# Normalising the probabilities of the first eight attention units on ScalarE and VectorE in place of GpSimd

## The chip, the core and the metric

The program runs on one core of a Trainium2 chip. The metric is the device time of one execution in microseconds (us). Five engines run their own queues in order: TensorE (PE; its weight loads are listed apart as PEld), VectorE (DVE), ScalarE (ACT), GpSimd (POOL) and SyncE (SP), which issues nearly all DMAs.

## What is computed

An attention with a forget gate, and two MLPs behind it, in float32:

```
attn:  scale*q@k.T + min(-(cum_i - cum_j), 0), causal, softmax, @ v      4 batches, 8 heads, 576 positions, 64 columns
x   -> moe:   g = s*relu(x@w_in)^2 + b;               x = g@w_out        2304 x 512, hidden 2048
x   -> moe2:  g = max(h,0) + alpha*min(h,0), h=x@w_in; out = g@w_out     2304 x 512, hidden 2048
```

`cum` is the running sum of max(s, 0). The softmax is `exp(scores - max) / (sum + 1e-9)`; the division is what the change moves.

## The kernel before

**Attention.** The work is cut into 32 units: a batch, a pair of heads, and one of two ranges of rows (rows 0 to 319 or 320 to 575). Range 0 has three row blocks, of 64, 128 and 128 rows with 64, 192 and 320 keys. Range 1 has two blocks of 128 rows, with 448 and 576 keys. The first eight units are called native: they use plain float32 matmuls. Units 0 to 3 (range 0 of batch 0) are early too: they borrow buffers of weights that are not there yet. Units 4 to 7 are range 1 of batch 0.

For each head of a unit `scores` fills the tile `probs` with the gate's bias (on ScalarE at L431 for the second head of a native unit, on VectorE at L435 for all others), masks it on GpSimd (L439), multiplies q and k (L457), combines score and bias with a running minimum or maximum on VectorE (L461), and takes the exponential on ScalarE with its sum (L473). Then VectorE adds 1e-9 and takes the reciprocal of the sums (L480, L481), and one GpSimd instruction for each row block scales `probs` by it in place (L484). `values` turns the scaled blocks with TensorE (L515, tile pt), copies them to `pf` (L519, on ScalarE and on VectorE), multiplies with v (L531) and copies the result into the MLP's input `xf` (L546, ScalarE).

**MLPs.** Each of the 16 packets of weights is converted from 64-bit to 32-bit numbers (L140 on ScalarE, L141 and L142 on VectorE) and split in a high and a low part (L130 on ScalarE, L131 on VectorE or GpSimd). A block of 256 tokens of the first MLP runs an up product (L783), the activation (L802 to L804, the split at L130 and L131) and a down product (L897) for each packet.

**Order.** The program starts with attention alone, up to the point where units 0 to 3 are done and unit 4 has begun. This stretch, some 62 us, is called the prelude here. In it TensorE also runs filler matmuls on zeros (`busy`, L97), which are kept at their place in the order. Then the first block of the MLP starts, and in it units 4 to 8 run beside the conversion of packets 4 to 15. Attention goes on beside later blocks until about 546 us; the second MLP takes the rest. The order on each engine is not that of the text: line 1047 asks for a planner that simulates the engines with its own costs and writes out each engine's queue from that. On the chip the queues run in that fixed order. Another mix of instructions gives another plan.

Of the kernel before, what the change touches and what calls it, by code (L numbers as in the profile page):

```python
# [12 lines left out]
AF = mybir.ActivationFunctionType  # L13
ALU = mybir.AluOpType
# [5 lines left out]
def tile_forget_attention__then__two_mlps(  # L20
# [20 lines left out]
    nc = tc.nc  # L41
# [52 lines left out]
    def busy(n):  # L94

        for _ in range(n):
            tc.keep_in_program_order(nc.tensor.matmul(scratch, dense[:, :P], dense, start=True, stop=True))  # L97
# [306 lines left out]
    def scores(u, h):  # L404

        own = HALF[h]
        head = u.b * H + u.h0 + h
        flip = u.native and h == 1
        nr = len(u.blocks)
        nm = two.tile([P, 3], F32, tag="nm", name=f"nm_{u.tag}_{h}")  # L410
        sm = two.tile([P, 3], F32, tag="sm", name=f"sm_{u.tag}_{h}")
        if u.rng == 0:
            nc.gpsimd.memset(sm[:, 0:1], 1.0)
        big = None if u.early else two.tile([P, 1088], F32, tag="probs", name=f"probs_{u.tag}_{h}")
        probs, col = {}, 0
        for r in u.blocks:
            i0, i1 = IB[r]
            rows = i1 - i0
            if u.early and r != 1:
                big, col = u.buf(two, 0, F32, "", f"probs{h}{r}"), 0  # L420

            width = -(-i1 // P) * P if i1 < S else S
            pt = probs[r] = big[:, col : col + width]
            col += width
            if width > i1:
                nc.gpsimd.memset(pt[:, i1:], 0.0)
            if r == 0:
                nc.gpsimd.memset(pt[64:P, 0:64], 0.0)

            if flip:  # L430
                nc.scalar.activation(  # L431
                    pt[:rows, :i1], u.cums[h][:rows, :i1], AF.Relu, scale=-1.0, bias=cumT[:rows, r, head : head + 1]
                )
            else:
                nc.vector.tensor_scalar(  # L435
                    out=pt[:rows, :i1], in0=u.cums[h][:rows, :i1], scalar1=cumT[:rows, r, head : head + 1],
                    scalar2=0.0, op0=ALU.subtract, op1=ALU.min,
                )
            nc.gpsimd.affine_select(  # L439
                out=pt[:rows, i0:i1], in_=pt[:rows, i0:i1], pattern=[[-1, rows]], base=0,  # L440
                channel_multiplier=1, compare_op=ALU.is_ge,
                fill=-MASKED if flip else MASKED,
            )
        u.probs[h] = probs
        for m, r in enumerate(u.blocks):
            i0, i1 = IB[r]
            rows, n = i1 - i0, i1
            a0 = i0 - u.q0
            pt = probs[r]
            init = -KEEP_ALL if flip else KEEP_ALL  # L450
            for j0, j1 in ([(0, n)] if n <= 512 else [(0, 320), (320, n)]):
                sc = u.bank("sc", f"sc{h}_{r}_{j0}")

                scr, all_ = sc[:rows, : j1 - j0], sc[:, : j1 - j0]
                aq = slice(a0, a0 + P)
                if u.native:
                    nc.tensor.matmul(all_, u.qk[0][own, aq], u.qk[1][own, j0:j1], start=True, stop=True)  # L457
                else:
                    nc.tensor.matmul(all_, u.xs[h][0][:, aq], u.xs[h][1][:, j0:j1], start=True, stop=False)
                    nc.tensor.matmul(all_, u.ql[h][:, aq], u.xs[h][1][:, j0:j1], start=False, stop=True)  # L460
                nc.vector.tensor_tensor_reduce(  # L461
                    out=pt[:rows, j0:j1], in0=scr, in1=pt[:rows, j0:j1], scale=SCALE if flip else -SCALE, scalar=init,
                    op0=ALU.subtract if flip else ALU.add, op1=ALU.max if flip else ALU.min,
                    accum_out=nm[:rows, m : m + 1],
                )
                if u.n < EARLY:
                    busy(1)
                init = nm[:rows, m : m + 1]
            if flip:
                nc.vector.tensor_scalar(  # L470
                    out=nm[:rows, m : m + 1], in0=nm[:rows, m : m + 1], scalar1=-1.0, scalar2=None, op0=ALU.mult
                )
            nc.scalar.activation(  # L473
                pt[:rows, :n], pt[:rows, :n], AF.Exp, bias=nm[:rows, m : m + 1], scale=1.0 if flip else -1.0,
                accum_out=sm[:rows, m : m + 1],
            )
            yield
        if u.n == 0:
            busy(4)
        nc.vector.tensor_scalar(out=sm[:, :nr], in0=sm[:, :nr], scalar1=1e-9, scalar2=None, op0=ALU.add)  # L480
        nc.vector.reciprocal(sm[:, :nr], sm[:, :nr])  # L481
        for m, r in enumerate(u.blocks):
            rows, n = IB[r][1] - IB[r][0], IB[r][1]
            nc.gpsimd.tensor_scalar(  # L484
                out=probs[r][:rows, :n], in0=probs[r][:rows, :n], scalar1=sm[:rows, m : m + 1],
                scalar2=1.0, op0=ALU.mult, op1=ALU.mult,
            )
        yield

    def values(u, h):  # L490
# [73 lines left out]
    def attention():  # L564
# [22 lines left out]
        for u in us:  # L587
            split_v(u)
        yield from transpose_qk(us[0])
        yield from alternate(transpose_qk(us[1]), scores(us[0], 0))  # L590
        yield from alternate(transpose_qk(us[2]), scores(us[0], 1))
        yield from alternate(transpose_qk(us[3]), scores(us[1], 0), values(us[0], 0))
        yield from alternate(scores(us[1], 1), values(us[0], 1))
        yield from alternate(scores(us[2], 0), values(us[1], 0))
# [457 lines left out]
```

## Time and profile before

| | |
|---|---|
| time, median of 3 runs | 1039.78 us (1039.27 to 1041.05) |
| the profiled execution | 1040.97 us; span from first to last instruction 1039.2 us |
| PE busy | 1019.4 us, 98% |
| DVE busy | 681.3 us, 66% |
| ACT busy | 672.4 us, 65% |
| POOL busy | 457.6 us, 44% |
| L484, POOL, whole execution | 160 instructions, 91.0 us |

Busy time is the sum of an engine's instructions. The idle time of an engine that is not the bottleneck costs nothing. "Idle before <- X" is the time in which an engine had nothing to run, and the instruction whose end let it go on. [...]

### The profile page before, as it was taken

What the parts mean: (1) busy time and instruction counts of PE and PEld (TensorE: products, weight loads), DVE (VectorE), ACT (ScalarE), POOL (GpSimd) and SP (SyncE); (2) the same over time, 40 slices, a digit from 0 to 9 for tenths busy, and PEclk for the clock granted to TensorE, in tenths of its full rate; (3) what the DMA queues carried; (4) which work ended last, traced back from release to release, by engine and by line L of the source; (5) the groups of instructions that cost most, each with busy time, mean ns of one, the idle gap of its engine ahead of it and who ended that gap; (6) DMA issues with size and microseconds to landing.
All of it is one profiled execution on the core that took longest, in us unless ns stands there. A gap on an engine that the chain in (4) does not pass through costs nothing. (4 is left out here: it accounts for less than half of the span.)

```text
span 1039.2 us, 20636 instructions
## 1 busy us (share of the span) xinstructions
PE 1019.4 (98%) x6952; PEld 925.8 (89%) x6952; DVE 681.3 (66%) x1605; ACT 672.4 (65%) x1669; POOL 457.6 (44%) x876
## 2 busy tenths in 40 slices
PE   9899999999999999999999999999999999999997
PEld 4568899999999999999999888888899999999996
DVE  6979865787676776677655865857665456455443
ACT  5877876777787877778776776645454455445433
POOL 5656775666677666777562000574611011001000
PEclk9999999999999999999999999999999999999999
DMA  7988433343232432334215762645644335334331
GB/s 167 255 211 239 132 68 70 71 93 79 40 92 64 102 72 52 79 68 91 66 35 173 240 192 74 207 147 170 196 163 142 103 112 172 103 99 136 104 104 46
DMA packets 197930, 125.45 MB, mean 121 GB/s; under 512 B 138496, under 2 KB 167936, under 8 KB 197824
## 3 DMA queue, kind: packets, MB, share of 16 engines
q1 hardware_dynamic: 193744, 123.56, 42.8%
q8 instruction: 55, 0.90, 0.4%
q10 hardware_dynamic: 4080, 0.57, 0.3%
q14 instruction: 51, 0.42, 0.1%
HBM read 106.19 MB, written 17.90 MB: 119 GB/s over the span
## 5 line engine op out<-in xcount | busy, mean ns | idle before, releaser
L783 PE MATMUL hp<-xh,w 128*128 128x256 f32 (+1 forms) x1024 | 229.0, 300 | 0.3 <-ACT r L802 0.3
L907 PE MATMUL acc<-w,ring 128*128 128x512 f32 x864 | 214.6, 392 | 1.1 <-DVE ring L131 0.7
L907 PEld LDWEIGHTS acc<-w,ring 128*128 128x128 f32 x864 | 155.8, 188 | 29.3 <-DVE ring L131 1.1
L783 PEld LDWEIGHTS hp<-xh,w 128*128 128x128 f32 x1024 | 171.4, 189 | 6.2 <-ACT r L802 0.5
L897 PE MATMUL acc<-gh,w 128*128 128x256 f32 x896 | 172.4, 286 | 0.5 <-ACT res L926 0.5
L783 PE MATMUL hp<-xl,w 128*128 128x256 f32 (+1 forms) x512 | 152.6, 298 | 0.0
L897 PEld LDWEIGHTS acc<-gh,w 128*128 128x128 f32 x896 | 136.0, 189 | 3.2 <-issue 1.6
L883 POOL TENSOR_TENSOR cc<-u,t 128x256 f32<-128x256 f32 x32 | 26.1, 817 | 235.5 <-DVE u L874 201.5
L897 PE MATMUL acc<-gl,w 128*128 128x256 f32 x448 | 118.7, 288 | 2.2 <-POOL gl L131 2.2
L484 POOL TENSOR_SCALAR probs<-probs,sm 64x64 f32<-64x64 f32 (+4 forms) x160 | 91.0, 581 | 60.5 <-DVE sm L481 49.9
L473 ACT ACTIVATE probs<-probs,nm 64x64 f32<-64x64 f32 (+4 forms) x160 | 90.0, 563 | 38.5 <-DVE nm L461 32.7
L131 POOL TENSOR_TENSOR gl<-r,gh 128x256 fp32r<-128x256 f32 x112 | 89.5, 799 | 48.6 <-ACT gh L130 42.1
L817 PE MATMUL p<-xs,sums 128*128 128x256 f32 x768 | 104.7, 282 | 0.4 <-DVE u L859 0.4
L783 PEld LDWEIGHTS hp<-xl,w 128*128 128x128 f32 x512 | 97.1, 190 | 3.3 <-issue 0.4
L817 PEld LDWEIGHTS p<-xs,sums 128*128 128x128 f32 x768 | 98.0, 189 | 2.1 <-DVE u L859 0.6
L461 DVE CUSTOM_DVE_ANT_0 probs<-sc,probs 128x320 f32<-128x320 f32 (+3 forms) x160 | 68.2, 427 | 41.2 <-PE sc L460 32.8
L817 PEld LDWEIGHTS p<-xs,w 128*128 128x128 f32 x576 | 79.0, 189 | 8.7 <-DVE u L874 2.0
L802 ACT ACTIVATE r<-hp 128x256 f32<-128x256 f32 (+1 forms) x144 | 58.0, 403 | 44.1 <-PE hp L783 33.2
L817 PE MATMUL p<-xs,w 128*128 128x256 f32 x576 | 82.3, 282 | 2.4 <-DVE u L874 1.5
L897 PEld LDWEIGHTS acc<-gl,w 128*128 128x128 f32 x448 | 80.1, 188 | 5.0 <-POOL gl L131 2.8
L828 DVE SCALAR_TENSOR_TENSOR ph<-pl,misc,ph 128x512 f32<-128x512 f32 x64 | 51.7, 807 | 42.4 <-ACT pl L844 42.4
L515 PE MATMUL pt<-ident,probs 128*128 128x128 f32 x480 | 74.3, 275 | 4.6 <-POOL probs L484 4.4
(149 smaller groups left out, 2116.8 us busy)
## 6 DMA issues: line engine op xcount, KB each, us to landing
sums<-sums_d SPq DMA_DIRECT2D x128, 256.0 KB, 2.7
wi<-in_moe_w_in_dram SPq DMA_DIRECT2D x32, 512.0 KB, 4.7
wo<-in_moe_w_out_dram SPq DMA_DIRECT2D x32, 512.0 KB, 4.8
cum<-cum_d SPq DMA_DIRECT2D x32, 288.0 KB, 3.7
sums_d<-w SPq DMA_DIRECT2D x64, 128.0 KB, 1.8
cum<-cum_d SPq DMA_DIRECT2D x30, 160.0 KB, 3.0
nat<-in_k_dram SPq DMA_DIRECT2D x64, 72.0 KB, 2.5
x_d<-res SPq DMA_DIRECT2D x18, 256.0 KB, 2.2
```

Of the source, the lines that this page charges most:

```text
L131: lo_eng.tensor_tensor(out=lo, in0=src, in1=hi.bitcast(F32), op=ALU.subtract)
L461: nc.vector.tensor_tensor_reduce(out=pt[:rows, j0:j1], in0=scr, in1=pt[:rows, j0:j1], scale=SCALE if flip else -SCALE, scalar=init, op0=AL ...
L473: nc.scalar.activation(pt[:rows, :n], pt[:rows, :n], AF.Exp, bias=nm[:rows, m : m + 1], scale=1.0 if flip else -1.0, accum_out=sm[:rows, m ...
L484: nc.gpsimd.tensor_scalar(out=probs[r][:rows, :n], in0=probs[r][:rows, :n], scalar1=sm[:rows, m : m + 1], scalar2=1.0, op0=ALU.mult, op1=A ...
L515: nc.tensor.transpose(tp[:, o : o + P], u.probs[h][r][:, k0 : k0 + P], ident)
L783: nc.tensor.matmul(hs, a[:, c], b[c], start=(n == 0), stop=(n == len(terms) * NCC - 1))
L802: relus.append(nc.scalar.activation(r, hs, AF.Relu, scale=1.0 / W_SCALE).ins)
L817: nc.tensor.matmul(bank, lhs[:, c * P : (c + 1) * P], rhs[:, c], start=(start and c == 0 and z == 0), stop=(c == 1 and z == 2), skip_group ...
L828: nc.vector.scalar_tensor_tensor(out=r, in0=u, scalar=nalpha[:, f : f + 1], in1=r, op0=ALU.mult, op1=ALU.add).ins
L883: nc.gpsimd.tensor_tensor(out=cc[:, T:], in0=u3, in1=t5, op=ALU.add)
L897: nc.tensor.matmul(banks[d] if count == 2 else acc[d // 2][:, d % 2], a[:, d * P : (d + 1) * P], b, start=(f == 0 and (d % 2 == 0 or count ...
L907: nc.tensor.matmul(banks[m], a[:, m * P : (m + 1) * P], b, start=(f == 0 and b is woh and a is gh), stop=(f == NF - 1 and a is gl),)
```

## The change

For native units, GpSimd's scaling is replaced: the first head of the pair (h = 0) is scaled by ScalarE with an activation (Copy with the reciprocal as a per-row scale), the second (h = 1) by VectorE with a tensor_scalar multiplication. All other units keep GpSimd.

```
         for m, r in enumerate(u.blocks):
             rows, n = IB[r][1] - IB[r][0], IB[r][1]
-            nc.gpsimd.tensor_scalar(
-                out=probs[r][:rows, :n], in0=probs[r][:rows, :n], scalar1=sm[:rows, m : m + 1],
-                scalar2=1.0, op0=ALU.mult, op1=ALU.mult,
-            )
+            pt, by = probs[r][:rows, :n], sm[:rows, m : m + 1]
+            if not u.native:
+                nc.gpsimd.tensor_scalar(out=pt, in0=pt, scalar1=by, scalar2=1.0, op0=ALU.mult, op1=ALU.mult)
+            elif h:
+                nc.vector.tensor_scalar(out=pt, in0=pt, scalar1=by, scalar2=None, op0=ALU.mult)
+            else:
+                nc.scalar.activation(pt, pt, AF.Copy, scale=by)
```

## Rows read from the trace of the kernel before

**Rows 1.** Busy time in stretches: start:end, length, each engine's busy (instructions), PEclk, DMA.
```profile
0.00:62.00 62.00, 55.52 (x227) 30.85 (x228) 48.27 (x159) 40.91 (x116) 35.95 (x112) 0.94 0.87 213
62.00:137.00 75.00, 73.80 (x490) 62.73 (x489) 67.11 (x138) 60.14 (x145) 49.99 (x73) 1.00 0.68 178
...
30.00:40.00 10.00, 9.33 (x38) 5.61 (x38) 9.47 (x34) 9.44 (x31) 5.19 (x12) 0.87 0.80 211
40.00:50.00 10.00, 8.85 (x44) 5.65 (x43) 9.56 (x30) 9.51 (x26) 5.29 (x9) 0.96 1.08 260
```
**Rows 2.** Timeline of PE around the prelude's end: start, length, instruction, [idle before].
```profile
53.76 0.55 PE L515 MATMUL pt<-ident,probs 128*128 128x128 f32 x3 [2.79 <-POOL probs L484]
...
60.51 1.30 PE L531 MATMUL av<-pf,vn 128*128 128x320 f32 x6
...
61.67 0.47 PE L783 MATMUL hp<-xh,w 128*128 128x256 f32 x1
```
**Rows 3.** Timeline of POOL, the scaling of four heads in the prelude.
```profile
23.34 1.53 POOL L484 TENSOR_SCALAR probs<-probs,sm 64x64 f32<-64x64 f32 x3 [0.72 <-DVE sm L481]
...
31.87 1.21 POOL L484 TENSOR_SCALAR probs<-probs,sm 64x64 f32<-64x64 f32 x3 [1.09 <-DVE nm L470]
...
34.55 1.57 POOL L484 TENSOR_SCALAR probs<-probs,sm 64x64 f32<-64x64 f32 x3 [1.15 <-DVE sm L481]
...
52.69 1.52 POOL L484 TENSOR_SCALAR probs<-probs,sm 64x64 f32<-64x64 f32 x3
```
**Rows 4.** Timeline of DVE, the reciprocal of unit 3's second head.
```profile
51.59 0.25 DVE L480 TENSOR_SCALAR sm<-sm 128x3 f32<-128x3 f32 x1
...
52.36 0.16 DVE L481 RECIPROCAL sm<-sm 128x3 f32<-128x3 f32 x1
```
**Rows 5.** Timeline of ACT: a trio and a pair at L431, an exponential's end.
```profile
14.22 1.15 ACT L431 ACTIVATE probs<-cum,cumT 64x64 f32<-64x64 f32 x3
...
47.08 0.19 ACT L473 ACTIVATION_READ_ACCUMULATOR probs<-probs,nm 128x1 f32 x1
...
72.64 1.34 ACT L431 ACTIVATE probs<-cum,cumT 128x448 f32<-128x448 f32 x2
```
**Rows 6.** Busy time of L484's instructions alone, in two stretches.
```profile
0.00:62.00 62.00, 13.00 (x26) 0.94 0.87 213
62.00:137.00 75.00, 12.40 (x14) 1.00 0.68 178
```
**Rows 7.** Timeline of DVE, multiplications of these shapes at L435.
```profile
13.70 1.66 DVE L435 TENSOR_SCALAR probs<-cum,cumT 64x64 f32<-64x64 f32 x3
...
23.41 1.64 DVE L435 TENSOR_SCALAR probs<-cum,cumT 64x64 f32<-64x64 f32 x3
...
26.71 2.68 DVE L435 TENSOR_SCALAR probs<-cum,cumT 64x64 f32<-64x64 f32 x3
...
65.44 0.86 DVE L435 TENSOR_SCALAR probs<-cum,cumT 128x448 f32<-128x448 f32 x2
...
154.46 0.77 DVE L435 TENSOR_SCALAR probs<-cum,cumT 64x64 f32<-64x64 f32 x3
```
**Rows 8.** Timeline of DVE, one instruction of the conversion, at three places.
```profile
32.29 1.08 DVE L141 TENSOR_SCALAR wt<-wt 128x512 uint32<-128x512 uint32 x1 [0.50 <-ACT wt L140]
...
35.50 0.90 DVE L141 TENSOR_SCALAR wt<-wt 128x512 uint32<-128x512 uint32 x1
...
43.55 0.39 DVE L141 TENSOR_SCALAR wt<-wt 128x512 uint32<-128x512 uint32 x1
```
**Rows 9.** PE alone in stretches of 2 us: busy, PEclk, DMA.
```profile
54.00:56.00 2.00, 2.00 (x10) 0.61 1.06 360
56.00:58.00 2.00, 2.00 (x8) 0.53 1.14 157
```
**Rows 10.** What L484 waited for in the prelude: us in total, times.
```profile
DVE sm L481: 7.2, 5
```
**Rows 11.** Table loads of ACT in the whole execution.
```profile
L84 ACT ACT_TABLE_LOAD x1 | 1.3, 1283 | 1.2 <-PEq L1034 1.2
```

## The prediction

> **What bounds the kernel now.** Read first the busy time in two stretches [rows 1]: the prelude (0 to 62 us) and the MLP's first block with units 4 to 7 beside it (62 to 137 us). From 62 us TensorE is busy for 73.80 of 75 us at full clock, and the whole span has it at 98%. So behind the prelude the kernel is bound by TensorE's own work, which the change leaves alone, and a microsecond is won there only by taking one of the 1.2 us of its idle time. The prelude is different: TensorE is idle for 6.5 us of it and spends much of the rest on filler matmuls. What lasts longest there is seen in its middle [rows 1]: from 30 to 50 us VectorE is busy for 19.03 us of 20 and ScalarE for 18.95, while GpSimd has 10.48.
>
> Read next, backwards from the first MLP matmul at 61.67 us, what TensorE did [rows 2]. Before it stands the product with v of unit 3's second head at 60.51. Earlier is the longest stall of the prelude: TensorE stood for 2.79 us, until 53.76, for GpSimd's scaling of that same head, and everything behind those transposes, the product of the first head included, stood with it. GpSimd had started at 52.69 [rows 3], at once behind the reciprocal that VectorE ran at 52.36 [rows 4]. VectorE ran the addition in front of it at 51.59, though ScalarE had finished that head's last exponential at 47.27, which is 47.08 + 0.19 [rows 5]: 4.3 us in VectorE's queue. The end of the prelude therefore hangs on two things, how long VectorE's queue takes to reach that reciprocal, and the scaling step behind it.
>
> **The change part by part.** *What GpSimd loses.* The scaling of units 0 to 7 is 13.0 us in the prelude and 12.4 us behind it [rows 6], 25.4 us in all, and none of it stands on GpSimd's own limit: that engine has idle time in both stretches.
>
> *The last scaling of the prelude (unit 3, second head) goes to VectorE.* Before, from the reciprocal's end (52.52) to the end of GpSimd's three instructions (52.69 + 1.52 = 54.21) was 1.69 us. The trace has no such multiplication by a reciprocal on VectorE. The nearest is L435, the same instruction type on the same three shapes, in and out of SBUF: 0.77 us for the trio where nothing slows it, 1.64 and 1.66 where GpSimd works beside it, 2.68 at worst [rows 7]. I take 0.77, because the GpSimd work that is removed is what often stood beside it, and because the row at 0.77 stands for 13 trios of that length in the trace. No semaphore of another engine stands between the reciprocal and this multiplication. The step gets shorter by 1.69 - 0.77 = 0.92 us. Bounds: 0.92 less, or 0.99 more (2.68).
>
> *VectorE's queue in front of it.* Three more second heads (units 0, 1, 2) are scaled before 52 us: 3 x 0.77 = 2.31 us longer. Against this stands what GpSimd's scaling costs VectorE today. L141 takes 0.39 us alone, and 1.08 and 0.90 while GpSimd scales from 31.87 to 33.08 and from 34.55 to 36.12 [rows 3, 8], 0.69 and 0.51 more. The trios of 1.66 and 1.64 us at L435 lie 0.89 and 0.87 above 0.77, the second beside the scaling at 23.34 [rows 3, 7]. These four places make 2.96 us. The queue is then 2.31 - 2.96 = 0.65 us shorter. GpSimd's other work moves into the room and will slow some of the same instructions, so I count half, 0.3 us shorter. Bounds: nothing removed and trios at 1.64 (4.9 us longer), or the whole 0.65 shorter.
>
> [...]
>
> *First heads go to ScalarE.* Nearest is L431, a ScalarE instruction on the same shapes with a per-row operand: 1.15 us for three blocks, 1.34 for two [rows 5]. Four trios make 4.6 us and four pairs 5.4. In the prelude unit 0's trio falls where ScalarE is idle; the trios of units 1, 2 and 3 go into the full queue, 3.45 us in front of the last exponential that now ends at 47.27. What hides it is the 4.3 us that this exponential's result lies in VectorE's queue; 0.85 us of that cover is left. If VectorE's queue got shorter by more than that, ScalarE would be late next, and the gain of the queue stops there. Unknown functions cost nothing: the trace has one table load in the whole execution [rows 11], and it already holds a plain copy beside the exponential.
>
> ScalarE also takes over the wait for the reciprocal. Queued behind it are exponentials, casts of weights and copies of pf; VectorE waits for the first two, TensorE for the last. I cost the wait at nothing, because the planner puts the scaling behind work that is ready; the second rival prices the opposite.
>
> *Behind the prelude.* Units 4 to 7 put 4 x 0.86 = 3.4 us on VectorE (the pair at 65.44 [rows 7]) and 4 x 1.34 = 5.4 us on ScalarE. Their idle time between 62 and 137 us is 75 - 67.11 = 7.9 us and 75 - 60.14 = 14.9 us [rows 1]; this covers both, and TensorE is fed from work done ahead. I cost it at nothing. Without that cover it would be up to 3.4 us. DMAs, their queues and their order in the text stay; the change issues none.
>
> *Sum.* -0.92 - 0.3 = -1.2 us. Against the profiled execution, 1040.97 us (span 1039.2 and 1.8 around it), that is 1039.8. The median of the runs lies 1.19 us below the profiled one, so I forecast 1039.78 - 1.2 = 1038.6 us.
>
> **The rivals.** A difference under 0.2% (2.1 us) is about what a measurement of this kernel can't tell from none.
>
> *The prelude's stall goes altogether (faster).* The planner writes the order anew. If it puts unit 3's addition and reciprocal 3 us nearer to the exponential, for which 4.3 us are there, the stall of 2.79 us is gone [rows 2]. [...] An engine that hasn't stood may keep its clock. Together 2.79 + 1.7 = 4.5 us: 1035.3. For it: VectorE's queue loses foreign waits, and two queues now hold the scaling that one held. Against it: the filler matmuls keep their places, and from 30 to 40 us, where TensorE is idle for 0.67 us alone, the granted clock is 0.87 too [rows 1].
>
> *ScalarE stands in front of the reciprocals (slower).* GpSimd waited five times for L481 in the prelude, 7.2 us in all, 1.44 each [rows 10]. It had nothing else to do; ScalarE has. If the plan places the scaling too early for units 1, 2 and 3, ScalarE stands 3 x 1.44 = 4.3 us between 23 and 47 us, with exponentials behind it. 0.85 us is covered, 3.4 is not, VectorE waits for the exponentials and gains nothing from its shorter instructions. -0.92 + 3.4 = +2.5 us: 1042.3. It decides from 0.85 + 0.92 = 1.8 us of waiting on. For it: ScalarE has 1.05 us of idle time in 20 [rows 1]. Against it: no planner that sees the reciprocal's time need put anything ahead of it.
>
> *The new multiplications are held as L435 is today.* Trios at 1.64 us: 3 x 1.64 - 2.96 = +2.0 us in the queue, and the last step 1.64 against 1.69. About +1.9 us: 1041.7. For it: two of the three prelude trios shown are at that price [rows 7]. Against it: 13 us of GpSimd's work are gone from the same stretch [rows 6].
>
> **How the numbers follow.** The forecast's case has 0.40, the case without the stall 0.35, ScalarE's waits 0.17, the held multiplications 0.08. Faster by over 0.2%: 0.35 and 0.02 from the edge of the forecast's case, 0.37. Slower: 0.17 and 0.01 from the edge of the held ones, 0.18. Within 0.2%: 0.38 and 0.07, 0.45. The range goes from 1034.8, half a microsecond under the case without the stall, to 1041.9, just above the held multiplications; it leaves out most of ScalarE's case. The forecast's own range is 1037.6 to 1040.2.
>
> **What the profile after would show.** The first L783 matmul at about 60.5 us instead of 61.67; L484 on GpSimd only from unit 8 on; trios near 0.8 us on VectorE and 1.15 on ScalarE; L141 nearer to 0.39 before 50 us; TensorE's stall in front of unit 3's second transposes under 2 us, now ended by VectorE; still about 1.2 us of idle time on TensorE between the prelude's end and 137 us. The prediction is wrong if the first L783 matmul comes after 62 us, if ScalarE waits for L481 for more than 1.8 us in the prelude, if the clock stays full through the prelude's end, or if the new plan moves idle time of TensorE into the first block or later ones.

## The result and the profile after

The changed kernel takes 1051.72 us in the median of 6 runs (1049.77 to 1054.42); the kernel before took 1039.88 beside it. The ratio is 1.0113 (1.0096 to 1.0131): 12 us slower, where 1.2 us less were forecast and the range ended at 1041.9. The profiled execution is 1052.57 us, span 1050.8. Lines behind L490 are shifted by 3: L518 is the transposes (L515 before), L522 the copy of pf (L519), L534 the product with v (L531), L786 and L900 the up and down products (L783, L897), L805 and L807 the activation (L802, L804). L490 is the scaling on ScalarE, L488 that on VectorE.

TensorE's timeline at the prelude's end in the changed kernel (start, length, instruction, [idle before]), to be set beside [rows 2]:

```profile
48.91 0.38 PE L97 MATMUL acc_first<-dense 128*128 128x512 bf16 x1
53.96 0.88 PE L518 MATMUL pt<-ident,probs 128*128 128x128 f32 x3 [4.67 <-ACT probs L490]
54.76 3.78 PE L457 MATMUL sc<-turned 64*128 64x448 f32 x6
...
68.14 1.20 PE L534 MATMUL av<-pf,vn 128*128 128x320 f32 x6
...
69.20 0.47 PE L786 MATMUL hp<-xh,w 128*128 128x256 f32 x1
```

The first up product starts 7.53 us later than in [rows 2]. TensorE goes on at nearly the same time as before (53.96 and 53.76), but it had waited for something else: for unit 3's *first* head, where before it was the second. All of unit 3's transposes and products then still lay ahead, and the six score matmuls of unit 4, which had run in front of the stall (at 49.01, in 1.96 us), came behind it and took 3.78 us.

Why the first head was late is seen on VectorE and ScalarE: the end of the first head's exponential, then the addition and the reciprocal (L480, L481), and the scaling. Before, the first head:

```profile
40.41 0.20 ACT L473 ACTIVATION_READ_ACCUMULATOR probs<-probs,nm 128x1 f32 x1
...
42.73 0.15 DVE L480 TENSOR_SCALAR sm<-sm 128x3 f32<-128x3 f32 x1
...
43.47 0.15 DVE L481 RECIPROCAL sm<-sm 128x3 f32<-128x3 f32 x1
```

After, ScalarE:

```profile
45.85 0.19 ACT L473 ACTIVATION_READ_ACCUMULATOR probs<-probs,nm 128x1 f32 x1
...
53.13 1.14 ACT L490 ACTIVATE probs<-probs,sm 64x64 f32<-64x64 f32 x3
```

After, VectorE (51.11 and 51.94 are the first head's, 52.60 and 52.79 the second's):

```profile
47.75 0.44 DVE L435 TENSOR_SCALAR probs<-cum,cumT 128x448 f32<-128x448 f32 x1
...
48.52 1.12 DVE L435 TENSOR_SCALAR probs<-cum,cumT 128x576 f32<-128x576 f32 x1
...
51.11 0.25 DVE L480 TENSOR_SCALAR sm<-sm 128x3 f32<-128x3 f32 x1
...
51.94 0.16 DVE L481 RECIPROCAL sm<-sm 128x3 f32<-128x3 f32 x1
...
52.60 0.15 DVE L480 TENSOR_SCALAR sm<-sm 128x3 f32<-128x3 f32 x1
...
52.79 0.17 DVE L481 RECIPROCAL sm<-sm 128x3 f32<-128x3 f32 x1
...
53.19 0.76 DVE L488 TENSOR_SCALAR probs<-probs,sm 64x64 f32<-64x64 f32 x3
```

The second head is where the forecast looked: its reciprocal comes at 52.79 instead of 52.36, its scaling ends at 53.95 instead of 54.21. The first head's reciprocal comes 8.47 us later (51.94 for 43.47). Of this, 5.4 us were there at its exponential's end (46.04 for 40.61). TensorE had stood twice by then, for a copy of pf on ScalarE and for L488, and the clock granted to TensorE, a share of full speed, was lower behind each (0.73 from 26 to 30 us; 0.75 from 34 to 36 and 0.50 from 36 to 38):

```profile
25.03 2.39 PE L534 MATMUL av<-pf,vn 128*128 128x320 f32 x6 [2.28 <-ACT pf L522]
...
33.75 0.85 PE L518 MATMUL pt<-ident,probs 128*128 128x128 f32 x6 [1.88 <-DVE probs L488]
```

The other 3 us went by in VectorE's queue, where two blocks of unit 4 are now filled with the gate's bias (L435) before this head's turn.

The windows of both kernels (start:end, length, busy of PE, PEld, DVE, ACT, POOL, PEclk, DMA share, GB/s; PEclk is that granted clock), before:

```profile
0.00:50.00 50.00, 46.30 (x192) 25.12 (x193) 40.15 (x135) 35.11 (x102) 29.00 (x102) 0.97 0.87 206
50.00:66.00 16.00, 13.21 (x63) 9.33 (x63) 10.99 (x32) 9.20 (x24) 8.62 (x15) 0.89 0.80 233
66.00:100.00 34.00, 33.92 (x213) 27.70 (x213) 31.08 (x66) 28.34 (x69) 21.75 (x30) 1.00 0.87 225
100.00:120.00 20.00, 18.88 (x130) 16.07 (x129) 18.93 (x32) 15.68 (x37) 14.05 (x17) 1.00 0.54 144
```

After:

```profile
0.00:50.00 50.00, 43.50 (x183) 24.61 (x183) 37.65 (x140) 36.07 (x105) 21.97 (x83) 0.93 0.85 208
50.00:66.00 16.00, 12.04 (x31) 6.90 (x31) 7.11 (x28) 9.09 (x25) 3.12 (x4) 0.57 0.80 226
66.00:100.00 34.00, 34.00 (x216) 27.87 (x214) 26.53 (x61) 23.98 (x58) 11.38 (x17) 1.00 0.61 149
100.00:120.00 20.00, 16.46 (x88) 13.40 (x87) 16.13 (x33) 16.80 (x40) 11.11 (x13) 0.84 0.62 201
```

TensorE's idle time in these stretches (length less busy) grows from 7.7 to 14.0 us, by 6.3. Clock lost, worked out as (1 - PEclk) x length, grows from 3.3 to 13.6, by 10.3; the two overlap where the clock is low while the engine stands, so they do not add up. Over the whole execution they can be told apart: TensorE's idle time grows from 19.8 to 24.8 us, and its busy time, for the same matmuls, from 1019.4 to 1026.0. So 5.0 of the 11.6 us of span are waits, and 6.6 are matmuls that ran longer. Two places stand out: the prelude's second half, at 0.57, and 100 to 120 us, where TensorE stood 1.12 us for an activation (L805), 1.82 for a cast on ScalarE (gh, L130), and again lost clock (0.50 from 114 to 120 us). Counted by the up products, the changed kernel is some 12 us behind from 120 us on, and the distance then hardly changes.

### The profile page after: what moved, and what is told of

It reads as the page before. It is cut to its first block, busy times and chain, and to the rows that moved or that the text cites. A ratio compares the mean times of both kernels' runs of the same rounds, so it can differ in the third digit from the quotient of the medians.

```text
span 1050.8 us, 20626 instructions
## 1 busy us (share of the span) xinstructions
PE 1026.0 (98%) x6952; PEld 931.1 (89%) x6952; DVE 676.8 (64%) x1625; ACT 681.7 (65%) x1689; POOL 434.8 (41%) x836
## 5 line engine op out<-in xcount | busy, mean ns | idle before, releaser
L786 PE MATMUL hp<-xh,w 128*128 128x256 f32 (+1 forms) x1024 | 230.0, 301 | 1.3 <-ACT r L805 1.1
L786 PEld LDWEIGHTS hp<-xh,w 128*128 128x128 f32 x1024 | 171.6, 190 | 8.1 <-ACT r L805 2.2
L900 PE MATMUL acc<-gh,w 128*128 128x256 f32 x896 | 171.5, 286 | 2.2 <-ACT gh L130 1.8
L786 PE MATMUL hp<-xl,w 128*128 128x256 f32 (+1 forms) x512 | 152.6, 298 | 0.0
L900 PEld LDWEIGHTS acc<-gh,w 128*128 128x128 f32 x896 | 136.1, 190 | 3.9 <-ACT gh L130 2.0
L900 PE MATMUL acc<-gl,w 128*128 128x256 f32 x448 | 117.8, 290 | 0.7 <-POOL gl L131 0.6
L131 POOL TENSOR_TENSOR gl<-r,gh 128x256 fp32r<-128x256 f32 x112 | 90.7, 809 | 59.3 <-ACT gh L130 52.7
L461 DVE CUSTOM_DVE_ANT_0 probs<-sc,probs 128x320 f32<-128x320 f32 (+3 forms) x160 | 68.3, 428 | 50.0 <-PE sc L460 28.2
L786 PEld LDWEIGHTS hp<-xl,w 128*128 128x128 f32 x512 | 97.3, 190 | 3.0 <-issue 0.3
L805 ACT ACTIVATE r<-hp 128x256 f32<-128x256 f32 (+1 forms) x144 | 58.2, 404 | 40.4 <-PE hp L786 32.0
L518 PE MATMUL pt<-ident,probs 128*128 128x128 f32 x480 | 76.6, 281 | 7.4 <-ACT probs L490 5.0
L900 PEld LDWEIGHTS acc<-gl,w 128*128 128x128 f32 x448 | 79.9, 190 | 2.8 <-POOL gl L131 2.7
L486 POOL TENSOR_SCALAR probs<-probs,sm 128x448 f32<-128x448 f32 (+3 forms) x120 | 64.5, 550 | 38.0 <-DVE sm L481 37.1
```

Source lines behind the costliest of these rows:

```text
L131: lo_eng.tensor_tensor(out=lo, in0=src, in1=hi.bitcast(F32), op=ALU.subtract)
L461: nc.vector.tensor_tensor_reduce(out=pt[:rows, j0:j1], in0=scr, in1=pt[:rows, j0:j1], scale=SCALE if flip else -SCALE, scalar=init, op0=AL ...
L486: nc.gpsimd.tensor_scalar(out=pt, in0=pt, scalar1=by, scalar2=1.0, op0=ALU.mult, op1=ALU.mult)
L518: nc.tensor.transpose(tp[:, o : o + P], u.probs[h][r][:, k0 : k0 + P], ident)
L786: nc.tensor.matmul(hs, a[:, c], b[c], start=(n == 0), stop=(n == len(terms) * NCC - 1))
L805: relus.append(nc.scalar.activation(r, hs, AF.Relu, scale=1.0 / W_SCALE).ins)
```

## The experiments

The ratio is to the kernel before, run again beside each experiment (its median there was 1038.9 to 1040.8 us). The columns on the right, the first up product's start and PEclk in three stretches, are of the one execution that was profiled. That is the slowest one in e6, e15 and e16, the fastest one in e5, e7, e11 and e12, and 3 us under the median in e3 and e4.

| run | what | median us | ratio (95%) | up product | 0:50 | 50:66 | 100:120 |
|---|---|---|---|---|---|---|---|
| before | | 1039.88 | | 61.67 | 0.97 | 0.89 | 1.00 |
| after | the change | 1051.72 | 1.0113 (1.0096 to 1.0131) | 69.20 | 0.93 | 0.57 | 0.84 |
| e1 | new engines, old order | 1044.62 | 1.0047 (1.0030 to 1.0063) | 64.50 | 0.93 | 0.89 | 1.00 |
| e2 | old engines, new order | 1051.96 | 1.0120 (1.0091 to 1.0148) | 68.87 | 0.93 | 0.68 | 0.81 |
| e3 | first heads only, own plan | 1048.76 | 1.0081 (1.0056 to 1.0107) | 66.52 | 0.83 | 0.90 | 1.00 |
| e4 | second heads only, own plan | 1046.27 | 1.0063 (1.0040 to 1.0087) | 61.91 | 0.90 | 0.89 | 1.00 |
| e5 | after, reciprocal early | 1048.11 | 1.0070 (1.0046 to 1.0094) | 65.00 | 0.93 | 0.79 | 0.83 |
| e6 | after, fillers in the stall | 1047.40 | 1.0072 (1.0048 to 1.0096) | 66.63 | 0.88 | 0.96 | 0.83 |
| e7 | both heads, old order, placed by hand | 1043.15 | 1.0023 (1.0007 to 1.0040) | 61.34 | 0.97 | 0.89 | 1.00 |
| e8 | second heads, the same | 1040.88 | 1.0010 (0.9992 to 1.0028) | 61.34 | 0.90 | 1.00 | 1.00 |
| e9 | after, wo early | 1051.45 | 1.0107 (1.0085 to 1.0130) | 69.17 | 0.91 | 0.75 | 0.83 |
| e10 | after, wo and reciprocal early | 1047.39 | 1.0069 (1.0046 to 1.0092) | 66.06 | 0.90 | 0.79 | 0.83 |
| e11 | before, fillers in its stall | 1038.93 | 0.9989 (0.9975 to 1.0003) | 59.76 | 0.97 | 1.00 | 1.00 |
| e12 | e8 with fillers | 1040.82 | 1.0004 (0.9992 to 1.0016) | 60.18 | 0.93 | 1.00 | 1.00 |
| e13 | after, gh early | 1051.62 | 1.0108 (1.0069 to 1.0146) | 70.92 | 0.83 | 0.71 | 0.87 |
| e14 | after, gh and reciprocal early | 1047.62 | 1.0068 (1.0046 to 1.0089) | 66.43 | 0.90 | 0.79 | 0.83 |
| e15 | old engines, new order to the up product | 1048.80 | 1.0088 (1.0065 to 1.0111) | 72.76 | 0.80 | 0.77 | 1.00 |
| e16 | old engines, new order behind it | 1046.59 | 1.0071 (1.0049 to 1.0093) | 60.42 | 0.93 | 0.98 | 0.83 |
| e17 | e8, copy early, fillers | 1041.92 | 1.0027 (1.0010 to 1.0044) | 61.74 | 0.90 | 0.89 | 1.00 |
| e18 | e7, copy early, fillers | 1041.44 | 1.0017 (1.0001 to 1.0033) | 60.09 | 1.00 | 0.89 | 0.91 |

### The order or the moved work (e1 to e4)

Theory A: the planner wrote another order for all engines, and that order costs. Theory B: the moved multiplications cost by their work. The plans differ in far more than the 40 moved instructions: 1,507 of TensorE's 6,838 instructions stand at another place, 378 of ScalarE's 1,521, 247 of VectorE's 1,413, 41 of SyncE's 691.

```
e1:  engines of the change; all queues but for the 40 moved instructions as the kernel before has them
e2:  engines of before;     all queues but for those 40 as the changed kernel has them
e3:  - if not u.native:    + if not u.native or h:        (GpSimd keeps the second heads)
e4:  - if not u.native:    + if not u.native or not h:    (GpSimd keeps the first heads)
```

> The scaling runs on ScalarE and VectorE as in the changed kernel, but every other instruction keeps the place in its engine's queue that it had before the change. If the new plan's order is what costs (theory A), the time is within 3 us of the kernel before, 1037 to 1043 us, with the first L786 matmul near 61 us and a mean granted clock near 0.995. If the moved work itself is what costs (theory B: ScalarE and VectorE are too full between 20 and 60 us), it is near the changed kernel, 1048 to 1053 us, with the first L786 matmul near 69 us.

> The scaling stays on GpSimd, but every other instruction takes the place in its queue that the changed kernel's plan gives it. Theory A (the order costs): near the changed kernel or slower, 1048 to 1056 us, clock near 0.986. Theory B (the moved work costs): near the kernel before, 1038 to 1043 us.

> Only the first heads are moved, to ScalarE; second heads stay on GpSimd; the planner is free. Theory B with ScalarE as the full engine: most of the 12 us, 1046 to 1052 us. Theory B with VectorE as the full engine: 1038 to 1042 us. Theory A: any value, by the plan that comes out, and the time then goes with the stalls and the granted clock of the prelude rather than with which half is moved.

> Only the second heads are moved, to VectorE; first heads stay on GpSimd; the planner is free. Theory B with VectorE as the full engine: 1046 to 1052 us. Theory B with ScalarE as the full engine: 1037 to 1042 us. Theory A: any value, by the plan that comes out.

e2 has nothing moved and loses the whole 12 us. TensorE waits in it for GpSimd's scaling (L484) where it waits for L488 and L490 in the changed kernel (until 34.35 and 54.45, there 33.75 and 53.96), and for gh as long as there; smaller waits differ. The largest up to 140 us (us in total, times, longest):

```profile
PE pt L515 <- POOL probs L484: 7.7, 2, 4.2
PE acc L897 <- ACT gh L130: 1.8, 1, 1.8
```

That GpSimd itself was slow in the new order is ruled out by its timeline. At both waits it began the scaling 0.1 us behind the reciprocal's end; at the second one:

```profile
52.84 0.16 DVE L481 RECIPROCAL sm<-sm 128x3 f32<-128x3 f32 x1
...
53.10 2.99 POOL L484 TENSOR_SCALAR probs<-probs,sm 64x64 f32<-64x64 f32 x6 [0.86 <-DVE sm L481]
```

So the order carries it: theory A. e1 loses 5 us all the same; there the planner still chose the places of the moved instructions, and TensorE waited 3.44 us until 56.62 for the last L488. e7 looks into whether that is place or work. e3 and e4, each with a plan of its own, are slower too; theory B had named 1046 to 1052 for whichever half carries the loss, and A any value, so they decide nothing.

### What the prelude's stall costs (e5, e6)

```
e5, after:  VectorE  L480, L481 (unit 3, first head) moved in front of the two L435
            ScalarE  its three L490 moved forward accordingly
e6, after:  TensorE  + 20 filler matmuls (L97) in front of unit 3's first transposes
```

> The changed kernel in its own order, with one place changed on two queues: the row sums' addition and reciprocal of unit 3's first head (L480, L481) go on VectorE in front of the two mask additions that stood before them, and that head's three multiplications (L490) go forward on ScalarE accordingly. Theory A (the new order costs: TensorE waits 4.67 us for this head at 53.96, and its half clock from 52 to 65 follows from that stall): the stall falls below 2 us, the granted clock of 54 to 64 is well over 0.5, the first matmul of the up product is back from 69.20 to about 63 to 65, and the time is about 1044 to 1048; what is lost in the first block (about 5 us from 101 to 120) stays. Theory B (the moved multiplications cost by the work they add to the two engines): the time stays near 1051, as the work is the same.

> The changed kernel in its own order, with 20 more of TensorE's filler matmuls (L97) put into the place where it stands still for 4.67 us before unit 3's first transposes; nothing else moves. If the clock that falls behind the stall is a cost of its own: the granted clock of 54 to 64 stays near 1.0, the six score matmuls that took 3.78 us there go back towards 1.96, and the first up product's matmul comes about 4 to 6 us earlier than at 69.20, so about 1046 to 1048 in all although the wait for the probabilities is as long as before. If the stall itself is the cost and the clock is only seen beside it: the landmark stays within 1 us of 69.20, or comes later by what of the fillers outlasts the stall, and the time stays at 1051 to 1053.

e5 gains 4.2 us at the up product and some 4 in the time, which ends at the slow edge of what was expected: the transposes ran at 49.74, but the next stall took the place, 2.86 us until 55.48 for VectorE's combination of scores (L461), with a clock of 0.50 until 60 us behind it. e6 tells what the clock is worth. TensorE's timeline in it:

```profile
52.47 4.70 PE L97 MATMUL acc_first<-dense 128*128 128x512 bf16 x21
57.01 0.49 PE L518 MATMUL pt<-ident,probs 128*128 128x128 f32 x3
57.43 1.99 PE L457 MATMUL sc<-turned 64*128 64x448 f32 x6
...
66.63 0.47 PE L786 MATMUL hp<-xh,w 128*128 128x256 f32 x1
```

The granted clock behind the fillers, of e6, and in the same place, of the changed kernel (busy, PEclk, DMA):

```profile
56.00:58.00 2.00, 2.00 (x11) 1.00 0.70 78
58.00:60.00 2.00, 2.00 (x11) 1.00 0.38 88
```

```profile
56.00:58.00 2.00, 2.00 (x5) 0.50 0.32 38
58.00:60.00 2.00, 2.00 (x7) 0.50 0.57 132
```

From those transposes to the up product the same instructions, without a wait in either, take 66.63 - 57.01 = 9.62 us, against 69.20 - 53.96 = 15.24. Half clock behind the stall costs 5.6 us, more than the stall. In e6 the transposes began 3 us later than in the changed kernel: the scaling itself came 2.4 us later (L490 at 55.51 for 53.13) in an execution that had lost clock earlier (0.55 from 44 to 50 us), and the fillers outlasted it by the rest. So 2.6 us are left at the up product, where 4 to 6 were expected; the time fell as expected.

### The arrangement that the prediction assumed (e7, e8)

```
e7:  engines of the change, every other instruction in the order of before;
     VectorE  L480, L481, + three L488 directly behind
     ScalarE  + L490 in front of the first instruction that began after that reciprocal in the trace of before
e8:  as e7, VectorE's half alone; first heads on GpSimd
```

> All eight units' multiplications on ScalarE and VectorE as in the changed kernel, with the order of every other instruction as in the kernel before, and the moved ones put by hand: VectorE's directly behind their reciprocal, ScalarE's in front of the first instruction that began after the reciprocal had ended in the trace of before. This is the arrangement that the prediction assumed. Theory A (only the places cost): the time is that of before or below, 1035 to 1041, with the first up product's matmul at 60 to 62.5. Theory B (the moved work costs wherever it stands): 1044 or more, as in the run with the old order and the planner's places (1044.6).

> Only the second heads' multiplications moved, to VectorE, each directly behind its reciprocal; the first heads' stay on GpSimd, and every other instruction keeps the order of before. Theory A: the last scaling of the prelude is shorter by about 0.9 us (0.77 for 1.69) and nothing else changes, so 1036 to 1040 and no stall longer than in before. Theory B: slower than before by the work added to VectorE's queue, 1042 or more.

With the old order most of the loss is gone: 12 us become 2.4 (0.7 to 4.2) with both heads moved, and 1.0 (-0.8 to 2.9) with the second heads alone. e7 lies between what the two theories expected, and the prediction's -1.2 did not come. Whether the 2.4 us that are left are the moved work or its place is not settled: the trace is of e7's fastest execution, which ends only 0.3 us of span behind the kernel before. VectorE in e7:

```profile
51.53 0.16 DVE L481 RECIPROCAL sm<-sm 128x3 f32<-128x3 f32 x1
...
51.73 0.84 DVE L488 TENSOR_SCALAR probs<-probs,sm 64x64 f32<-64x64 f32 x3
...
52.50 0.67 DVE L131 TENSOR_TENSOR w<-wt,w 128x512 fp32r<-128x512 f32 x1
...
53.10 0.21 DVE L522 COPY pf<-pt 128x64 f32<-128x64 f32 x1
```

and TensorE:

```profile
53.45 0.52 PE L518 MATMUL pt<-ident,probs 128*128 128x128 f32 x3 [3.38 <-DVE pf L522]
...
61.34 0.47 PE L786 MATMUL hp<-xh,w 128*128 128x256 f32 x1
```

The scaling ended at 52.57, 1.64 us earlier than before: the reciprocal came 0.83 us earlier, where 0.3 was forecast, and the step behind it took 0.88 us for 1.69, about as sized. But TensorE was let go only 0.31 us earlier (53.45 for 53.76), by the copy of pf, which reads the buffer pt that these transposes write. In the kernel before the copy ran from 53.05 to 53.26, 0.74 us behind the reciprocal's end and half a microsecond ahead of the stall's end. In e7 the scaling stands between the two, and the copy ends 1.62 us behind the reciprocal's end: what the scaling won, the copy behind it lost again. Behind the stall the clock was 0.50 from 54 to 56 us.

### The first block (e9, e10, e13 to e16)

```
e9,  after:  SyncE    wo of packet 9 in front of eight nat loads and one of cum
e10, after:  e9 and e5
e13, after:  ScalarE  gh (L130) directly behind its square (L807), six places forward
e14, after:  e13 and e5
```

> The changed kernel in its own order, with one DMA issue moved on SyncE's queue: the tenth slab of the weights wo is issued in front of the eight loads of nat and the one of cum behind which the new plan had put it (92.40 in the trace of after). If the 5 us lost in the first block come from that place (ScalarE stands 3.28 us for this slab at 99.47, the activations behind it come late, and TensorE stalls 1.12 and 1.82 and runs at half clock from 112 to 120): the wait of ScalarE and both stalls go, the clock of 100 to 120 is above 0.95, the gap to before stays near the 7.5 us that it has at the first up product, and the time is 1045.5 to 1048. If the loss comes from ScalarE's extra work there (L490 at 1.33 a pair): the stalls stay and the time is within 1 us of 1051.7.

> The edits of the two runs before put together: unit 3's first reciprocal early on VectorE and its multiplications early on ScalarE, and the tenth wo slab in front of the nat loads. If the two places are separate causes, their gains add: 3.6 (measured for the first) and about 4 to 6 for the second, so 1042 to 1044.5. If one is a consequence of the other, the sum is no better than the better one alone, 1046 or more.

> The changed kernel in its own order, with one instruction moved on ScalarE: the cast gh (L130) of the first block's seventh slab directly behind the square (L807) that it reads, in place of behind two weight casts, an exponential, two copies and the cast xh (112.20 in the trace of after, where the square had ended at 109.27). If that place costs the 5 us of the first block: TensorE's stall of 1.82 in front of 112.65 goes, the clock of 110 to 120 is near 1.0 instead of half for most of it, the gap to before no longer grows between the 84th and the 96th up product (it grew from 5.1 to 10.8), and the time is 1045.5 to 1048. If TensorE there waits for whatever comes last in a stretch in which three engines are late together: another wait of 1 us or more takes the place, and the time is 1050 or more.

> That cast early and unit 3's first reciprocal and multiplications early, the two edits together. If these two places with the clock behind them carry the 12 us: 1040.5 to 1043.5, near the kernel before. If many places of the new order each carry a little: 1045 or more.

In all four the time expected first did not come, and the rival's did. e9 removed most of ScalarE's wait for wo (0.3 us for 3.28) and TensorE's of 1.12, and TensorE's wait for gh stayed, 2.0 us. The cause that e9's rival named, ScalarE's extra work, does not follow from this, since e2 loses as much without it. e13 removed the wait for gh, and one for ScalarE's scaling took its place. TensorE's waits from 92 to 120 us, of e9 and then of e13:

```profile
PE acc L900 <- ACT gh L130: 2.0, 1, 2.0
```

```profile
PE pt L518 <- ACT probs L490: 2.1, 1, 2.1
```

The clock was 0.50 behind each (114 to 118 us in e9, 116 to 120 in e13), and the time stayed. e10 and e14 gain no more than e5 alone. So neither of these two late instructions is the cause there by itself; e15 and e16 then split the order itself.

```
e15:  kernel before; queues up to the first up product as in the changed kernel, behind it as before
e16:  kernel before; queues up to the first up product as before, behind it as in the changed kernel
```

> The kernel before, multiplications on GpSimd, with the changed kernel's order of every queue up to the first up product and the order of before behind it. If the order of the first block is a cost of its own: TensorE's waits and half clock of 100 to 120 go (idle below 1.5 us, clock above 0.95, where the run with the new order throughout had 2.6 idle and 0.81), the prelude's 7 us stay, and the time is 1046 to 1048. If the first block only suffers from the late prelude: the waits stay in another place and the time is 1050 to 1053.

> The kernel before, multiplications on GpSimd, with its own order up to the first up product and the changed kernel's order behind it. If the order of the first block is a cost of its own: the first up product comes at 61.7 as in before, the waits and the half clock of 100 to 120 are there, and the time is 1043.5 to 1046. If the loss there came from the prelude's lateness: no such stretch, and 1039 to 1042.

The window of 100 to 120 us, of e15 and of e16:

```profile
100.00:120.00 20.00, 20.00 (x132) 16.66 (x131) 19.40 (x39) 16.47 (x39) 13.46 (x19) 1.00 0.75 213
```

```profile
100.00:120.00 20.00, 15.58 (x87) 13.42 (x87) 16.09 (x33) 14.20 (x33) 13.65 (x18) 0.83 0.59 174
```

With the new prelude alone TensorE never stands there, though its first up product comes later than in any other run; with the new rest alone it stands 4.4 us at 0.83. The loss of the first block belongs to its own order and not to a late prelude. How large it is cannot be read from e16: the two parts are not additive (0.88% and 0.71% against 1.20% together in e2), and e16 lost clock where neither the kernel before nor the changed one did (0.81 from 66 to 100 us), behind 1.5 us of idle time from 62 to 66 us, at the seam of the two orders. Its trace is also the slowest of executions from 1042.98 to 1050.17 us.

### Can the stall be won (e11, e12, e17, e18)

```
e11:  before:  TensorE + 11 fillers in front of unit 3's second transposes, - 3 of the 4 behind them
e12:  e8:      TensorE +  9 there,                                        - 3 of 4
e17:  e8:      TensorE +  6 there, - 3 of 4; VectorE: the copy of pf in front of L480
e18:  e7:      the same two edits
```

> The kernel before, order and engines unchanged, except TensorE's fillers (L97): 11 are put into its stall of 2.79 us in front of 53.76, and 3 of the 4 that stood behind it go. If half clock behind a stall is a cost of its own: the clock of 54 to 58 is near 1.0 instead of 0.61 and 0.53, the stretch from the stall's end to the first up product falls from 7.9 us to 5 to 5.5, that product begins near 59 instead of 61.67, and the time is 1036.5 to 1039. If not, the stretch loses only the three fillers (0.6 us) and the time stays within 1 us of before.

> The second heads' multiplications on VectorE directly behind their reciprocals, all else in the order of before, and TensorE's fillers moved: 9 in front of unit 3's second transposes, 3 of the 4 that stood behind them gone. The candidate to beat both kernels: the first up product near 58.5 to 60 and the time 1036 to 1039. If moving the multiplications is worth nothing beside the fillers, it equals the kernel before with fillers; if the place costs something on VectorE, it is slower than that one.

> Second heads on VectorE behind their reciprocals, first heads on GpSimd, the order of before, and two places moved: the last copy of pf of unit 3's first head goes in front of the addition and reciprocal of its second head, and 6 filler matmuls stand in TensorE's stall in front of that head's transposes, with 3 of the 4 behind them gone. If the copy was what took the place of the scaling: TensorE is let go by L488, at 52 to 52.8 us in a trace like that of before, the first up product comes at 58.5 to 59.5, and the time is 1036 to 1038.5. If yet another wait follows: the first up product is no earlier than with the fillers alone (59.8) and the time is 1039 to 1041.

> The same two places moved, with both heads' multiplications on ScalarE and VectorE at the places by hand. If ScalarE's multiplications cost nothing where they stand: equal to the run with the second heads alone, 1036 to 1038.5. If they cost in ScalarE's queue: 1 to 2.5 us more than that run, as the two kernels without these edits stood (1043.15 and 1040.88).

e11 shows the clock's part once more. TensorE in it goes on at 53.80, as in [rows 2], but at full clock, and reaches the up product 5.96 us later instead of 7.91; the clock of 54 to 58 is 1.00 where [rows 9] have 0.61 and 0.53:

```profile
50.94 2.55 PE L97 MATMUL acc_first<-dense 128*128 128x512 bf16 x11
53.80 0.55 PE L515 MATMUL pt<-ident,probs 128*128 128x128 f32 x3 [0.32 <-POOL probs L484]
...
59.76 0.47 PE L783 MATMUL hp<-xh,w 128*128 128x256 f32 x1
```

The gain at the up product is 1.9 us; about 0.6 of it are the three fillers that went. The ratio, 0.9989 (0.9975 to 1.0003), does not tell it from no change. e12 was to beat both kernels at 1036 to 1039 and did not (1040.82): with the fillers, the moved second heads bring nothing on top. e18 shows what became of the wait once the copy was out of the way too. TensorE in it:

```profile
51.58 0.52 PE L518 MATMUL pt<-ident,probs 128*128 128x128 f32 x3 [0.98 <-DVE probs L488]
...
56.07 0.33 PE L518 MATMUL pt<-ident,probs 128*128 128x128 f32 x1 [1.45 <-ACT probs L490]
...
60.09 0.67 PE L786 MATMUL hp<-xh,w 128*128 128x256 f32 x1
```

TensorE is let go 2.2 us earlier than in [rows 2], now by the scaling itself, and then waits 1.45 us for unit 4's first head, at a clock of 0.50 from 58 to 60 us. In e17 the same wait came, 0.98 us until 57.77 for GpSimd's scaling of that head, so the rival expectation held there (yet another wait; 1041.92, a little over its 1039 to 1041). e18 equals e17 (1041.44 and 1041.92): ScalarE's half adds nothing that could be measured there. Neither is faster than the kernel before, and no arrangement tried beats it by more than a measurement can tell.

## Why the prediction was wrong

**The step that failed** is that the sum was made in the order of the kernel before: "VectorE's queue in front of it" reckons the instructions of that order as if they stayed where they were, and the part behind the prelude says that DMAs, "their queues and their order in the text stay". The order in the text did stay, but the planner wrote all five engines' queues anew, SyncE's too, and the new order alone costs the whole 12 us (e2). A new order of everything else was priced only as a way to be faster. The forecast followed one head, the one that ended last; the new plan made the other head last, 8.5 us later than before.

**The last scaling** was sized rightly: 0.76 us in the changed kernel and 0.84 in e7, against 0.77. Its worth was not: the whole arrangement of e7 brought 0.31 us at TensorE, where 0.92 were forecast for this step alone, since the copy of pf behind it ended the stall. What else would end the stall was not looked for. The 0.92 was also reckoned to the end of GpSimd's third block (54.21), while TensorE went on at 53.76, as soon as the second was done (53.70 in the trace of before).

**VectorE's queue.** Between 20 and 50 us L141 mostly took 0.38 to 0.42 us, as said, but 1.53 (37.12) and 1.22 (42.64) where GpSimd's splits (L131) ran beside it. The gain did not show at the end, since the queue held other work.

**ScalarE's step and its wait.** The trio took 1.14 us and the pair 1.33, as taken from [rows 5]. Its wait "at nothing, because the planner puts the scaling behind work that is ready" came true to the letter: ScalarE waited 0.5 us for a reciprocal in the whole execution. Readiness for ScalarE was bought with lateness for TensorE, which stood 4.67 us for that scaling. The rival in which ScalarE stands in front of the reciprocals is thereby wrong as well; that its sign was right is luck.

**The held multiplications** did not come in the prelude, where all four trios took 0.76 or 0.77 us. Behind it, one pair of the four took 0.88 us (70.44), as forecast, and the others 1.90 (96.72), 1.91 (126.74) and 1.34 (146.09). GpSimd ran L131 beside these three, from 96.94 to 98.30, from 126.23 to 127.96 and from 146.02 to 146.75. That the two went together is all that the runs show; why these three took longer is not shown. The pairs came to 6.0 us in place of 3.4, but they are not what costs the 12 us: e2, where none of them is on VectorE, loses as much.

**Behind the prelude** was costed at nothing, on the idle time of two engines. Two of the signs that the prediction named for being wrong came true: the first up product after 62 us (69.20), and idle time of TensorE moved into the first block (3.5 us from 100 to 120 us, for 1.1). The second had no chance and no price of its own. What that order does wrong is not settled: every edit of one place (e9, e13) brought the next wait in. In the changed kernel ScalarE and VectorE are busy 4.4 and 4.6 us less from 66 to 100 us than before, and are late behind. Counted from the first matmul of the up products to the 85th, ScalarE is busy for 31.0 us and VectorE for 32.2, against 34.8 and 36.6 before; e2, which loses in the first block too, has 29.7 and 31.1, and e15, which loses nothing there, has 34.4 and 36.9. So the loss goes with work left undone there; that it is the cause is not shown.

**The clock** was counted as something to win (1.7 us, in the first rival), not to lose. No run shows these 1.7 us, an estimate from the clock in [rows 9], (1 - 0.61) x 2 + (1 - 0.53) x 2: with that stall filled, e11 had a clock of 1.00 from 54 to 58 us and was 1.9 us earlier at the up product, about 0.6 of which were the fillers that went. A clock of 0.50 behind one longer stall, of 4.67 us, cost 5.6 us (e6 against the changed kernel).

## What to carry to other kernels

Where a planner writes the queues, a change of an instruction's engine is two changes. Measure the new order by itself, by running the old engines in the new order and the new engines in the old one. Before a stall is counted as won, look for what else ends within its length on the same queues; here a copy ended 0.5 us before it, and the next unit's scaling came after that (e7, e18). Where TensorE bounds the kernel, reckon a stall together with the clock behind it (here 5.6 us behind a stall of 4.67), and try filler work in it before anything is rearranged. Here that took 4 us off the changed kernel (e6), but nothing that could be measured off the kernel before (e11).

## What the runs showed of the hardware

In the changed kernel a wait of 4.67 us, until 53.96, was followed by a granted clock of 0.50 from 54 to 64 us, though TensorE was busy for all of these 10 us; it was 0.57 from 64 to 66 us and 1.00 from 66 to 100. With filler matmuls in the wait the clock behind it was 1.00 (52 to 64 us in e6, 54 to 58 in e11). The times of the changed kernel spread with that clock: its six executions run from 1049.77 us at a mean clock of 0.988 to 1054.42 at 0.983, and 0.5% of 1050 is 5.3 us.
